# Stage one's products and stage two's token tiles of neighbouring batches, alternated one by one in the source

## The chip, the cores and the metric

The kernel runs on one core of a Trainium2 chip. The metric is the device time of one execution in microseconds (us); lower is better. TensorE (PE) multiplies into PSUM, VectorE (DVE), ScalarE (ACT) and GpSimd (POOL) work on the results, and SyncE (SP) issues the transfers. Each engine runs its own list of instructions in the list's order and waits on semaphores for the others.

## The reference, cut to what matters

Block-sparse attention over 4 batches of 768 tokens, then a mixture of 8 experts in which every token passes through every expert, with weights that a balancing loop makes:

```python
x = attention(q, k, v, sampled_blocks)          # 3072 tokens x 512
logits = x @ w_gate
P = np.exp(logits - logits.max())
for _ in range(8):                              # balance rows and columns
    P /= P.sum(1, keepdims=True) + 1e-09
    P /= P.sum(0, keepdims=True) + 1e-09
    P *= N / E
for e in range(E):                              # 8 experts
    h = np.maximum(x @ w1[e], 0.0)              # 512 -> 1024
    ye = h @ w2[e]                              # 1024 -> 512
    out += P[:, e:e + 1] * ye
```

## The kernel before, in words

The first 420 us or so are the attention. The rest is the experts, and the change is there. Every operand is held as a high and a low half in 16 bits, so that a product of two numbers takes three matmuls (high by low, low by high, high by high), and both matrix products of an expert are done by a scheme of seven products (`NP = 7`) of quarter matrices in place of eight.

The work goes by 32 steps `i`, an expert and a batch of 768 tokens each (`e, b = divmod(i, 4)`). A step has two stages.

- **Stage one** (`stage1(i, qi)`, `qi` from 0 to 3, a quarter each): seven products p0, p1, p5, p6, p3, p4, p2 in this order, each of six matmuls of 384 columns (L1200) into one of four PSUM banks (`ps_h`). DVE or ACT takes a product out of its bank: ACT for p0 (L1247), DVE for the others (`comb`, L1212, twice for p4). The results a1, r11, u3, c21 are made positive on ACT, added and subtracted on POOL (L1274, L1086), and split by `emit` into tiles for h: a high half by ACT (L1222), then a low half by DVE or POOL (L1226, L1232). There are 30 buffers for h; a step fills 28.
- **Stage two** (`stage2(i, p)`): for each of the seven products, in the order 1, 0, 5, 6, 3, 4, 2, three token tiles of twelve matmuls of 256 columns (L1325) into PSUM banks of another pool of four (`ps_y`). DVE (or ACT, for some of the first expert) adds each tile to the sum in SBUF (L1349, L1346). Products 5 and 6 go on in the bank of product 0, and 2 in that of 4, so DVE must have read a bank before the next product adds to it. A tile of stage two reads h of all four quarters.

In the names of the order below, `p3_12_0` is product 3 of step 12, quarter 0; `py_12_1_0` is the bank of stage two's product 1 of step 12, token tile 0; `h_24`, `acc_0`, `w2p_1` are buffers.

Stage one of step i+1 and stage two of step i have nothing to do with each other, and PE gets both. In the kernel before the source puts them in turns of whole blocks: stage two's products 1 and 0 (six tiles), quarter 0 (seven products), product 5 (three tiles), quarter 1, products 6 and 3, quarter 2, products 4 and 2, quarter 3.

Two things decide the order on each engine besides the source. `Slots` queues the small work of the other engines (high and low halves, weight splits) and places it by estimated costs at each `tick`, which comes after every product and every token tile. And the framework's scheduler then orders the instructions of each engine by its own estimate of when each will be ready, so that blocks of the source can be taken apart.

**The changeover.** After the fourth batch of an expert the weights of the next one take the place of the old ones. `split_w1` queues ACT's high halves (L1064) and DVE's low halves (L1068) of the seven w1 matrices at the last quarter of the last batch; `load_w(2, e + 1)` loads w2 (2 MB) into the buffer that w1 has just left, `scale_w` finds its largest magnitude in eight parts on ACT (L108) and a scale, and `split_w2` queues the halves (L1064, L1068) and POOL's sums (L1079). Steps 3, 7, 11, ... (b = 3) and the step after each are the changeover; in steps with b = 1 and 2 no weights are split.

Of the kernel before, what the change touches and what calls it, by code (L numbers as in the profile page):

```python
# [20 lines left out]
P = 128  # L21
# [19 lines left out]
PRE, LB2, LB1 = 0, 1, 1  # L41
# [13 lines left out]
def tile_sparse_attention_moe(  # L55
# [12 lines left out]
    B, H, S, D = q.shape  # L68
    NT, DM = out.shape
    NE, _, FF = w1.shape  # L70
# [6 lines left out]
    KF = FF // P  # L77
# [4 lines left out]
    FH = FF // 2  # L82
    CH = NC // 2
    TH = S // 2
    NP = 7
# [85 lines left out]
    wr = {}  # L171
# [879 lines left out]
    slots = Slots()  # L1051
# [131 lines left out]
    hs = {}  # L1183
# [7 lines left out]
    def stage1(i, qi, used=None):  # L1191
# [16 lines left out]
        def fresh(nm):  # L1208
            return upool.tile([P, TH], F32, tag="u", name=f"{nm}_{i}_{qi}")

        def comb(t, ps, other):
            nc.vector.scalar_tensor_tensor(  # L1212
                out=t, in0=ps, scalar=HDOWN, in1=other, op0=ALU.mult, op1=ALU.add
            )

        def emit(p, src, relu=False, delay=0):
            h = hfree.pop(0)
            hs[i, p, qi] = h
            key = ("h", i, p), i, qi

            def high():
                nc.scalar.activation(h[:, 0], src, AF.Relu if relu else AF.Copy)  # L1222

            def low():
                if relu:
                    nc.vector.scalar_tensor_tensor(  # L1226
                        out=h[:, 1], in0=src, scalar=0.0, in1=h[:, 0],
                        op0=ALU.max, op1=ALU.subtract,
                    )
                else:  # L1230
                    eng = nc.gpsimd if p in lop else nc.vector
                    eng.tensor_tensor(out=h[:, 1], in0=src, in1=h[:, 0], op=ALU.subtract)  # L1232
# [12 lines left out]

        a1 = fresh("a1")
        nc.scalar.activation(a1, product(0), AF.Copy, scale=HDOWN)  # L1247
# [7 lines left out]
        tick(1, 0)  # L1255
        u3 = fresh("u3")
        comb(u3, product(6), a1)
        tick(1, 0)
        slots.settle(i, qi - 1)
        c21 = fresh("c21")  # L1260
        comb(c21, product(3), u3)
        emit(1, c21, relu=True)
        tick(1, 1)
        p5 = product(4)
        comb(u3, p5, u3)
        comb(a1, p5, a1)
        nc.scalar.activation(u3, u3, AF.Relu)
        emit(3, u3)
        tick(2, 2)
        comb(a1, product(2), a1)  # L1270
        nc.scalar.activation(a1, a1, AF.Relu)  # L1271

# [13 lines left out]
        emit(5, r11, delay=SD[2])  # L1286
        emit(2, c21, delay=SD[3])
        tick(1, 1)

    READS = {  # L1290
        1: ((0, 0),),
# [12 lines left out]
    def stage2(i, p):  # L1304
        e, b = divmod(i, B)
# [8 lines left out]
        for ci in range(CH):  # L1314
# [63 lines left out]
    stage1(0, 0)  # L1378
    for part in split_w2(0, wr[2]):
        part()  # L1380
    stage1(0, 1)
    stage1(0, 2)
    stage1(0, 3)
    load_x(1)
    for step in xlast:
        slots.add(step, ("late", 0, 0), LATE, True, dve=1.0, act=0.8, pool=0.8)
    balance()
    queue_weight(0)
    for i in range(NI):
        e, b = divmod(i, B)  # L1390
        nxt = e + 1 < NE
        last = b == B - 1 and nxt
        more = i + 1 < NI
        if i == 2:
            finish_late()

        def quarter(qi):
            if more:
                swap = qi == FH // P - 1 and b == B - 2 and nxt
                stage1(i + 1, qi, split_w1(e + 1) if swap else None)  # L1400

        if b == LB2 and nxt:
            for p in range(NP):
                slots.need(("w2", e, p))
            if PRE:
                load_w(2, e + 1)
                scale_w(2, e + 1)
        if b == LB1 and nxt:
            slots.need(("scale", 2, e + 1))
            load_w(1, e + 1)  # L1410
            scale_w(1, e + 1)
            sum_w1(e + 1)
        stage2(i, 1)
        stage2(i, 0)
        if last:
            for p in range(NP):
                slots.need(("w1", e + 1, p))
            load_w(2, e + 1)
            parts = split_w2(e + 1, wr[2])
            scale_w(2, e + 1)  # L1420
            parts[0]()
            queue_weight(e + 1)
        quarter(0)
        stage2(i, 5)
        if last:
            parts[1]()
        quarter(1)
        stage2(i, 6)
        stage2(i, 3)
        if last:  # L1430
            parts[2]()
        quarter(2)
        stage2(i, 4)
        stage2(i, 2)
        if last:
            parts[3]()
        quarter(3)
        if i + 2 < NI:
            load_x(i + 2)

# [29 lines left out]
```

## Time and profile before

| | us |
|---|---|
| median of 3 runs | 2243.07 |
| their range | 2240.85 to 2245.97 |
| the profiled execution, whole | 2243.44 |
| its span, first to last instruction | 2241.5 |
| busy: PE / DVE / ACT / POOL | 2167.8 / 1696.3 / 1319.2 / 1320.5 |
| granted TensorE clock | 0.998 |

The table's busy times are unions of the instructions' spans. A matmul's span includes the way through the array, so a PE row that counts as busy is not necessarily at full rate; the rate is read from the distance between starts. "Idle before" in the views of PE is the time from the modelled end of a matmul to the start of the next.

### The profile page before, as it was taken

Reading aid. Unit: us, or ns where it says so; the run is one execution under the profiler, and the core shown is the slowest. Engines: PE = TensorE matmul, PEld = TensorE weight load, DVE = VectorE, ACT = ScalarE, POOL = GpSimd, SP = SyncE. Lnnn points to the kernel's source line nnn. Section 1 sums busy time; section 2 is a strip of 40 time slices with the busy share of each in tenths; the row PEclk is TensorE's granted clock in tenths of the full one; section 3 lists DMA queues with packets and bytes.
Section 4 is the critical chain, followed back from the end, with each engine's and each line's share of the span. In section 5 each row is a group of like instructions: output and inputs, shape, how many; then the busy total and the mean of one; then the engine's idle time right before and its main releaser. Section 6 shows DMA issues by size and latency. Waiting matters only on the chain.

```text
span 2241.5 us, 47250 instructions
## 1 busy us (share of the span) xinstructions
PE 2167.8 (97%) x18892; PEld 1598.0 (71%) x18892; DVE 1696.3 (76%) x2989; ACT 1319.2 (59%) x2443; POOL 1320.5 (59%) x1369
## 2 busy tenths in 40 slices
PE   6999999889999999999999999999999999999999
PEld 4777667567677777677767776777677767776777
DVE  7889999777877667866786678767876787678765
ACT  6988889764566555554555455545554555455442
POOL 3124456595568564856585658565856585658553
PEclk9999999999999999999999999999999999999999
DMA  7666866313121212121212121212121212121221
GB/s 166 141 147 148 206 130 145 116 57 116 50 88 51 88 50 88 50 88 50 88 50 88 51 88 50 88 50 88 50 88 50 88 50 88 50 88 57 78 79 50
DMA packets 195345, 192.35 MB, mean 86 GB/s; under 512 B 132124, under 2 KB 150580, under 8 KB 195124
## 3 DMA queue, kind: packets, MB, share of 16 engines
q1 hardware_dynamic: 194560, 189.30, 29.5%
q8 instruction: 147, 2.41, 0.4%
q14 instruction: 74, 0.61, 0.1%
q10 hardware_dynamic: 564, 0.03, 0.0%
HBM read 140.54 MB, written 17.30 MB: 70 GB/s over the span
## 4 chain that ended last, share of the span: by engine, by line
PE 60%; DVE 13%; POOL 10%; ACT 8%; issue 5%; DMA 4%; DVEq 0%; SPq 0%; POOLq 0%; ACTq 0%
PE py L1325 25%; PE p L1200 24%; DMA r<-in_moe_w_dram 3%; PE u L760 3%; POOL r L1079 2%; ACT h L1222 2%; DVE top L678 2%; PE t L705 2%; PE m L669 2%; PE m L672 2%; PE t L702 2%; POOL s L1274 2%; ACT unread L108 2%; POOL h L1232 2%; DVE attic L1068 1%
## 5 line engine op out<-in xcount | busy, mean ns | idle before, releaser
L1325 PE MATMUL py<-w2p,h 128*128 128x256 f16 x8064 | 952.5, 273 | 12.7 <-DVE acc L1349 4.6
L1325 PEld LDWEIGHTS <-h 128*128 128x128 f16 x8064 | 787.8, 98 | 154.6 <-issue 17.1
L1232 POOL TENSOR_TENSOR h<-u,h 128x384 f16<-128x384 f32 x128 | 124.8, 975 | 559.1 <-ACT h L1222 559.1
L1200 PEld LDWEIGHTS <-attic 128*128 128x128 f16 x3072 | 299.5, 98 | 206.1 <-issue 24.5
L1200 PE MATMUL p<-attic 128*128 128x384 f16 x2304 | 412.3, 326 | 16.5 <-DVE a L1212 10.2
L1200 PE MATMUL p<-arena 128*128 128x384 f16 x2304 | 416.3, 327 | 2.2 <-DVE u L1212 1.0
L1349 DVE SCALAR_TENSOR_TENSOR acc<-py,spare,acc 128x256 f32<-128x256 f32 (+1 forms) x588 | 295.3, 515 | 144.9 <-PE py L1325 142.8
L1222 ACT ACTIVATE h<-c 128x384 f16<-128x384 f32 x256 | 132.8, 522 | 320.4 <-DVE c L1212 262.8
L1200 PEld LDWEIGHTS <-arena 128*128 128x128 f16 x2304 | 225.8, 98 | 130.7 <-issue 4.6
L1212 DVE SCALAR_TENSOR_TENSOR a<-p,a 128x384 f32<-128x384 f32 x384 | 211.6, 551 | 22.6 <-PE p L1200 16.7
L678 DVE TENSOR_REDUCE top<-m 128x1 f32<-128x768 f32 x192 | 182.0, 952 | 31.2 <-PE m L672 30.8
L710 ACT ACTIVATE pe<-t,qk 128x768 int32<-128x768 f32 x192 | 172.1, 899 | 45.1 <-PE t L705 42.2
L1222 ACT ACTIVATE h<-s 128x384 f16<-128x384 f32 x128 | 67.1, 524 | 174.6 <-POOL s L1274 174.6
L1222 ACT ACTIVATE h<-r 128x384 f16<-128x384 f32 x256 | 131.7, 521 | 61.8 <-POOL r L1086 58.9
L1232 DVE TENSOR_TENSOR h<-s,h 128x384 f16<-128x384 f32 x128 | 105.5, 824 | 80.6 <-ACT h L1222 80.6
L1086 POOL TENSOR_TENSOR r<-s,r 128x384 f32<-128x384 f32 x128 | 154.0, 1203 | 10.0
L1086 POOL TENSOR_TENSOR c<-c,r 128x384 f32<-128x384 f32 x128 | 151.1, 1181 | 10.0
L1200 PE MATMUL p<-arena,attic 128*128 128x384 f16 x768 | 146.2, 326 | 5.5 <-ACT a L1247 4.7
L1274 POOL TENSOR_TENSOR s<-a,u 128x384 f32<-128x384 f32 x128 | 140.9, 1101 | 16.7 <-ACT a L1271 16.6
L1232 POOL TENSOR_TENSOR h<-r,h 128x384 f16<-128x384 f32 x128 | 134.7, 1052 | 18.3 <-ACT h L1222 16.3
L1079 POOL TENSOR_TENSOR r<-r 128x256 f32<-128x256 f32 (+1 forms) x106 | 119.1, 1148 | 30.9 <-DVE arena L1068 30.9
L669 PE MATMUL m<-kt,qt 128*128 128x512 f16 (+1 forms) x384 | 127.8, 333 | 9.0 <-DMA kt<-ks 6.8
(205 smaller groups left out, 3671.8 us busy)
## 6 DMA issues: line engine op xcount, KB each, us to landing
arena<-xd SPq DMA_DIRECT2D x128, 384.0 KB, 3.9
attic<-xd SPq DMA_DIRECT2D x96, 384.0 KB, 4.2
r<-in_moe_w_dram SPq DMA_DIRECT2D x16, 2048.0 KB, 8.6
arena<-in_q_dram SPq DMA_DIRECT2D x16, 384.0 KB, 4.0
arena<-in_k_dram SPq DMA_DIRECT2D x16, 384.0 KB, 4.3
arena<-in_v_dram SPq DMA_DIRECT2D x4, 1536.0 KB, 8.3
xd<-xs_t SPq DMA_DIRECT2D x16, 384.0 KB, 3.1
out_dram<-acc SPq DMA_DIRECT2D x48, 128.0 KB, 1.7
```

Source lines behind the costliest of these rows:

```text
L669: nc.tensor.matmul(sc[:, lo:hi], lhsT=qt[:, 0, c], rhs=ka[:, lo:hi], start=True, stop=False)
L678: nc.vector.tensor_reduce(out=tops[n][:, c : c + 1], in_=sc[:, :S], axis=AX.X, op=ALU.max)
L710: nc.scalar.activation(pe, sc[:, :S], AF.Exp, bias=EXP_SHIFT, scale=qk[n // 2][3])
L1079: lambda c=c: Pinned.gpsimd.tensor_tensor(out=out[:, c], in0=x[:, c], in1=y[:, c], op=op),
L1086: nc.gpsimd.tensor_tensor(out=out, in0=x, in1=y, op=ALU.subtract)
L1200: nc.tensor.matmul(ps, lhsT=w1p[p][:, l, kc, fs], rhs=xp[p][:, r, kc], start=(kc == 0 and m == 0), stop=(kc == KH - 1 and m == 2),)
L1212: nc.vector.scalar_tensor_tensor(out=t, in0=ps, scalar=HDOWN, in1=other, op0=ALU.mult, op1=ALU.add)
L1222: nc.scalar.activation(h[:, 0], src, AF.Relu if relu else AF.Copy)
L1232: eng.tensor_tensor(out=h[:, 1], in0=src, in1=h[:, 0], op=ALU.subtract)
L1274: nc.gpsimd.tensor_tensor(out=s1, in0=a1, in1=u3, op=ALU.add)
L1325: nc.tensor.matmul(py, lhsT=hs[i, p, kc][:, l, tsl], rhs=w2p[p][:, r, kc], start=(old is None and kc == 0 and m == 0), stop=(kc == KF // 2 ...
L1349: nc.vector.scalar_tensor_tensor(out=dst, in0=src, scalar=c, in1=dst, op0=ALU.mult, op1=ALU.add)
```

## The change

`stage1` and `stage2` become generators that yield after each product and each token tile. The loop over the steps starts stage two's tiles of step i three tiles ahead (`LEAD = 3`), and then takes products of step i+1 and tiles of step i in turn, 28 products against the 18 tiles that are left. The order of the products within each stage is what it was. The new weights' work hangs on the generators: w2's load stands after the sixth tile and the product that precedes the seventh, which makes seven products ahead of it in the source where there were none. The buffers for h are taken from the list when the high half is made, not when it is queued, and are given back after the last tile of a product.

```diff
         def emit(p, src, relu=False, delay=0):
-            h = hfree.pop(0)
-            hs[i, p, qi] = h
             key = ("h", i, p), i, qi
 
             def high():
+                h = hs[i, p, qi] = hfree.pop(0)
                 nc.scalar.activation(h[:, 0], src, AF.Relu if relu else AF.Copy)
 
             def low():
+                h = hs[i, p, qi]
...
         nc.scalar.activation(a1, product(0), AF.Copy, scale=HDOWN)
         tick(0, 1)
+        yield
         r11 = fresh("r11")
...
             slots.tick(1.31, 0.47 if k is not None else 0.74)
-        for kc in range(KF // 2):
-            hfree.append(hs.pop((i, p, kc)))
+            if ci == CH - 1:
+                for kc in range(KF // 2):
+                    hfree.append(hs.pop((i, p, kc)))
+            yield
...
+    ORDER2 = (1, 0, 5, 6, 3, 4, 2)
+    LEAD = 3
...
+    def products(i):
+        e, b = divmod(i, B)
+        for qi in range(FH // P):
+            swap = qi == FH // P - 1 and b == B - 1 and e + 1 < NE
+            yield from stage1(i, qi, split_w1(e + 1) if swap else None)
+
+    def outputs(i):
+        e, b = divmod(i, B)
+        last = b == B - 1 and e + 1 < NE
+        for n, p in enumerate(ORDER2):
+            yield from stage2(i, p)
+            if last and n == 1:
+                for x in range(NP):
+                    slots.need(("w1", e + 1, x))
+                load_w(2, e + 1)
+                parts = split_w2(e + 1, wr[2])
+                scale_w(2, e + 1)
+                parts[0]()
+                queue_weight(e + 1)
+            elif last and n in (2, 4, 6):
+                parts[n // 2]()
...
-        stage2(i, 1)
-        stage2(i, 0)
-        if last:
-            for p in range(NP):
-                slots.need(("w1", e + 1, p))
-            load_w(2, e + 1)
...
-        quarter(0)
-        stage2(i, 5)
...
-        quarter(3)
+        two = outputs(i)
+        if i + 1 == NI:
+            run(two)
+            break
+        one = products(i + 1)
+        n1, n2 = NP * FH // P, NP * CH
+        for n in range(LEAD):
+            next(two)
+        done = 0
+        for n in range(n1):
+            next(one)
+            want = (n + 1) * (n2 - LEAD) // n1
+            for _ in range(want - done):
+                next(two)
+            done = want
+        run(one)
+        run(two)
         if i + 2 < NI:
             load_x(i + 2)
```

What the scheduler makes of it, on the engines for which PE waits in the changeover to expert 3 (steps 11 to 13). Up to the middle of step 1 PE's list is the same row for row. From there on, of the 672 tiles of stage two, 598 stand in one piece on PE, where 431 did, and PE's list changes between products and tiles 1125 times, where it did 825 times. All instructions are the same in number and shape.

ACT's list in step 12, from the search for w2's largest magnitude (`unread`) to the drain of p0 of quarter 2 (`a1_12_2<-p0_12_2`), before:

```order
L108 ACTIVATE unread_80,mx_w2_3_15976<-r2_3_15973 128x512 x2
L1222 ACTIVATE h_21_8093<-s1_12_1_16180 128x384
L1222 ACTIVATE h_4_8076<-a1_12_1_16104 128x384
L1222 ACTIVATE h_15_8087<-r11_12_1_16116 128x384
L1222 ACTIVATE h_13_8085<-c21_12_1_16149 128x384
L1247 ACTIVATE a1_12_2_16277<-p0_12_2_16278 128x384
```

And the same place now:

```order
L108 ACTIVATE unread_80,mx_w2_3_16052<-r2_3_16049 128x512
L1277 ACTIVATE a1_12_1_16070<-a1_12_1_16070 128x384
L1247 ACTIVATE a1_12_2_16226<-p0_12_2_16227 128x384
L1221 ACTIVATE h_1_8073<-s1_12_1_16205 128x384
L108 ACTIVATE unread_80,mx_w2_3_16052<-r2_3_16049 128x512
L1221 ACTIVATE h_3_8075<-a1_12_1_16070 128x384
```

The drain of p0 stood behind four high halves, which take POOL's results of the quarter before; it now stands ahead of them.

DVE's list in step 13, quarter 1, around the drain of p5 (`a1_13_1<-p5_13_1`), before:

```order
L1212 SCALAR_TENSOR_TENSOR r11_13_1_16790<-p1_13_1_16791,a1_13_1_16777 128x384
L1232 TENSOR_TENSOR h_14_8086<-a1_13_0_16648,h_14_8086 128x384
L1068 SCALAR_TENSOR_TENSOR w2p_4_8069<-t1_3_15975,sw2_3_15978,w2p_4_8069 128x1024
L1349 SCALAR_TENSOR_TENSOR acc_0_8102<-py_12_0_0_16601,spare_6_16491,acc_0_8102 128x256
L1232 TENSOR_TENSOR h_7_8079<-r11_13_1_16790,h_7_8079 128x384
L1349 SCALAR_TENSOR_TENSOR acc_0_8102<-py_12_0_1_16617,spare_6_16491,acc_0_8102 128x256
L1349 SCALAR_TENSOR_TENSOR acc_0_8102<-py_12_0_2_16632,spare_6_16491,acc_0_8102 128x256
L1212 SCALAR_TENSOR_TENSOR a1_13_1_16777<-p5_13_1_16801,a1_13_1_16777 128x384
```

And now:

```order
L1068 SCALAR_TENSOR_TENSOR w2p_5_8070<-r2_3_16049,sw2_3_16054,w2p_5_8070 128x1024
L1212 SCALAR_TENSOR_TENSOR r11_13_1_16773<-p1_13_1_16774,a1_13_1_16746 128x384
L1212 SCALAR_TENSOR_TENSOR a1_13_1_16746<-p5_13_1_16787,a1_13_1_16746 128x384
L1232 TENSOR_TENSOR h_5_8077<-s1_13_0_16724,h_5_8077 128x384
L1212 SCALAR_TENSOR_TENSOR u3_13_1_16810<-p6_13_1_16811,a1_13_1_16746 128x384
```

Six rows stood between the drains of p1 and p5, a weight split and three additions of tiles among them; now none does.

DVE's list at the start of step 13, where the first weights that stage two of expert 3 needs are split (`w2p_1`), before:

```order
L1212 SCALAR_TENSOR_TENSOR a1_12_3_16455<-p2_12_3_16528,a1_12_3_16455 128x384
L1068 SCALAR_TENSOR_TENSOR w2p_1_8066<-r2_3_15973,sw2_3_15978,w2p_1_8066 128x1024
L1212 SCALAR_TENSOR_TENSOR r11_13_0_16658<-p1_13_0_16659,a1_13_0_16648 128x384
L1212 SCALAR_TENSOR_TENSOR a1_13_0_16648<-p5_13_0_16671,a1_13_0_16648 128x384
```

And now:

```order
L1356 SCALAR_TENSOR_TENSOR acc_3_9931<-py_11_4_2_16428,spare_5_13892,acc_3_9931 128x256
L1212 SCALAR_TENSOR_TENSOR r11_13_0_16612<-p1_13_0_16613,a1_13_0_16603 128x384
L1232 TENSOR_TENSOR h_24_8096<-s1_12_3_16523,h_24_8096 128x384
L1212 SCALAR_TENSOR_TENSOR a1_13_0_16603<-p5_13_0_16639,a1_13_0_16603 128x384
L1068 SCALAR_TENSOR_TENSOR w2p_1_8066<-r2_3_16049,sw2_3_16054,w2p_1_8066 128x1024
```

The split of `w2p_1` has moved from ahead of step 13's first drains to behind those of p1 and p5. On PE the first tiles that read it stood behind four products of step 13, and stand behind six now. On ACT, 110 of the high halves carry a wait for PE (for the last reads of the buffer's old content), where 61 did.

More of the change, by code (lines that the diff above doesn't have):

```diff
@@ L1253, in stage1 @@
         tick(1, 2)
+        yield
         comb(a1, product(5), a1)
         tick(1, 0)
+        yield
         u3 = fresh("u3")
@@ L1258, in stage1 @@
         tick(1, 0)
+        yield
         slots.settle(i, qi - 1)
@@ L1263, in stage1 @@
         tick(1, 1)
+        yield
         p5 = product(4)
@@ L1269, in stage1 @@
         tick(2, 2)
+        yield
         comb(a1, product(2), a1)
@@ L1288, in stage1 @@
         tick(1, 1)
+        yield
     READS = {
@@ L1377, in tile_sparse_attention_moe, with run @@
     NI = NE * B
-    stage1(0, 0)
+    ORDER2 = (1, 0, 5, 6, 3, 4, 2)
+    LEAD = 3
+    def run(steps):
+        for _ in steps:
+            pass
+    run(stage1(0, 0))
     for part in split_w2(0, wr[2]):
         part()
-    stage1(0, 1)
-    stage1(0, 2)
-    stage1(0, 3)
+    for qi in range(1, FH // P):
+        run(stage1(0, qi))
     load_x(1)
@@ L1391, in tile_sparse_attention_moe @@
         nxt = e + 1 < NE
-        last = b == B - 1 and nxt
-        more = i + 1 < NI
         if i == 2:
             finish_late()
[L1397 to L1400, printed above, removed]
         if b == LB2 and nxt:
```

20 lines of the change are left out of this document (1 added, 19 removed).

## The prediction, as it was put on record before the run

> **What bounds the kernel now.** The page's head and first row come first.
>
> ```profile
> span 2241.5 us, 47250 instructions
> PE 2167.8 (97%) x18892; PEld 1598.0 (71%) x18892; DVE 1696.3 (76%) x2989; ACT 1319.2 (59%) x2443; POOL 1320.5 (59%) x1369
> ```
>
> PE is the bound, but 97% doesn't say at what rate it works. The timeline of PE in a step without weight work (start, length, engine, line, instruction, count) gives the rate by the distance between starts.
>
> ```profile
> 779.82 6.28 PE L1325 MATMUL py<-w2p,h 128*128 128x256 f16 x56
> 785.93 3.09 PE L1200 MATMUL p<-arena 128*128 128x384 f16 x18
> 788.86 1.14 PE L1200 MATMUL p<-arena,attic 128*128 128x384 f16 x6
> 789.83 0.71 PE L1325 MATMUL py<-w2p,h 128*128 128x256 f16 x5
> 790.38 3.09 PE L1200 MATMUL p<-attic 128*128 128x384 f16 x18
> ```
>
> 56 matmuls of a tile take 785.93 - 779.82 = 6.11 us, 0.109 each; 18 of products take 2.93, 0.163 each. So a product of six costs 0.98 us and a tile of twelve 1.31. The last two rows tell what a change of stage costs: five matmuls of a tile between two products take 0.55, 0.110 each, so nothing. Next the windows view, 110 us each, two without weight work (the first and the last) and two changeovers.
>
> ```profile
> core 0: us, PE busy (x) PEld busy (x) DVE busy (x) ACT busy (x) POOL busy (x), PEclk, DMA share, GB/s
> 755.00:865.00 110.00, 110.00 (x846) 82.54 (x845) 74.57 (x138) 60.26 (x123) 65.26 (x63) 1.00 0.16 52
> 865.00:975.00 110.00, 106.86 (x808) 78.57 (x806) 87.02 (x150) 65.39 (x129) 76.16 (x73) 1.00 0.22 74
> 1090.00:1200.00 110.00, 106.68 (x809) 78.48 (x807) 87.02 (x150) 61.71 (x122) 78.02 (x73) 1.00 0.22 76
> 1202.00:1312.00 110.00, 110.00 (x847) 82.60 (x845) 73.64 (x137) 53.76 (x112) 64.28 (x62) 1.00 0.16 53
> ```
>
> Without weight work PE never stands: nothing can be won there. A changeover has 38 matmuls fewer in the same time, which at 110 / 846 = 0.13 us each is 4.9 us lost, although DVE is busy for 87.0 of 110 us only. So these are waits, not a full engine. The list of PE's waits from 865 us on (us in total, times, longest) names them.
>
> ```profile
> PE p L1200 <- DVE a L1212: 8.0, 6, 1.3
> PE p L1200 <- ACT a L1247: 4.7, 5, 0.9
> PE py L1325 <- DVE acc L1349: 4.6, 10, 1.0
> PE p L1200 <- ACT attic L1064: 2.3, 5, 0.5
> PE py L1325 <- DVE h L1226: 1.2, 6, 0.2
> PE p L1200 <- ACT arena L1064: 0.5, 1, 0.5
> PE p L1200 <- DVE r L1212: 0.4, 1, 0.4
> ```
>
> Most are waits for a PSUM bank that DVE or ACT has not emptied in time (a, acc, r: 17.7 us, 22 times); weights come next (attic, arena: 2.8, 6 times), and low halves of h (1.2, 6 times). The view counts from the modelled end of a matmul, and that is late: a product's last matmul lasts 1.14 - 5 x 0.163 = 0.33 us where the next may follow after 0.163. Each wait is thus about 0.16 us longer than shown.
>
> The same wait, in the same step of two changeovers five apart, gives the whole loss:
>
> ```profile
> 947.17 1.14 PE L1200 MATMUL p<-attic 128*128 128x384 f16 x6 [1.33 <-DVE a L1212]
> ...
> 2071.21 0.97 PE L1200 MATMUL p<-attic 128*128 128x384 f16 x5 [1.34 <-DVE a L1212]
> ```
>
> (2071.21 - 947.17) / 5 = 224.8 us per expert. Its work is four steps of 168 matmuls of products and 252 of tiles: 672 x 0.1628 + 1008 x 0.1091 = 219.4. So 5.4 us are lost per changeover, and six changeovers from 865 us on hold 32.5. Of these the waits explain 17.7 + 22 x 0.16 = 21.2 for banks, 2.8 + 6 x 0.16 = 3.8 for weights, 1.2 + 6 x 0.16 = 2.2 for h; 5.3 are left for waits too short to show.
>
> **The change, part by part.** *Banks.* Two changeover waits, one on ACT and one on DVE:
>
> ```profile
> 1124.41 1.20 POOL L1086 TENSOR_TENSOR c<-c,r 128x384 f32<-128x384 f32 x1
> ...
> 1125.64 0.52 ACT L1222 ACTIVATE h<-c 128x384 f16<-128x384 f32 x1 [0.75 <-POOL c L1086]
> 1126.07 0.47 ACT L1247 ACTIVATE a<-p 128x384 f32<-128x384 f32 x1
> ...
> 1126.59 0.97 PE L1200 MATMUL p<-arena,attic 128*128 128x384 f16 x5 [0.94 <-ACT a L1247]
> ```
>
> ACT drains p0 only after four high halves that wait for POOL, and p6, which needs that bank, stands for 0.94 + 0.16 = 1.1 us. In the new order the drain is ahead of those halves: its own 0.47 us is all that is left. Besides, between p0 and p6 there is now a tile of 1.31 us, so the same lateness of 1.1 would be covered even without the move. The wait on DVE is alike:
>
> ```profile
> 1164.67 0.90 DVE L1232 TENSOR_TENSOR h<-s,h 128x384 f16<-128x384 f32 x1 [2.90 <-ACT h L1222]
> ...
> 1166.77 2.01 DVE L1068 SCALAR_TENSOR_TENSOR w2p<-t,sw,w2p 128x1024 f16<-128x1024 f32 x1
> ...
> 1170.68 0.54 DVE L1212 SCALAR_TENSOR_TENSOR a<-p,a 128x384 f32<-128x384 f32 x1
> ```
>
> p5's drain starts at 1170.68 behind a low half, a weight split and three tiles; it now follows the drain of p1 directly. PE meets the banks with four products in a row (3 x 0.98 = 2.9 us between a bank's uses) in the old order and mostly with one or two tiles among them (4.2 to 5.6) in the new. Bounds: at most all 21.2 us go, at least those at the two shown places (6 and 5 of the 22, 8.0 + 4.7 + 11 x 0.16 = 14.5) shrink by half, 7. I take 19 of 21.2, near the upper end, because both the order and the distance help. The low half of h that stage two's first tile waits for comes from p3 of the last quarter; between the two PE now has two tiles of the old step more (2.6 us) against waits of 0.2 + 0.16 each: 2.2 go, or none.
>
> *Weights.* The waits for w1 I leave as they are, since an old matrix still can't be overwritten before its last product: 3.8 stay (0 to 8). Where the new w2p_1 is read, a wait could appear: with 0 at the start of step 13, p1 ends at 1.95, and DVE then does a drain, a low half, a drain and the split. The rows for these, with that of a tile's addition (by shape; the mean of one in ns is the second number behind the first bar):
>
> ```profile
> L1349 DVE SCALAR_TENSOR_TENSOR acc<-py,spare,acc 128x256 f32<-128x256 f32 x504 | 233.8, 477 | 139.4 <-PE py L1325 137.2 <-ACT acc L1333 1.5
> L1212 DVE SCALAR_TENSOR_TENSOR a<-p,a 128x384 f32<-128x384 f32 x384 | 211.6, 551 | 22.6 <-PE p L1200 16.7
> ...
> L1232 DVE TENSOR_TENSOR h<-s,h 128x384 f16<-128x384 f32 x128 | 105.5, 824 | 80.6 <-ACT h L1222 80.6
> ...
> L1068 DVE SCALAR_TENSOR_TENSOR w2p<-r,sw,w2p 128x1024 f16<-128x1024 f32 x48 | 66.1, 1379 | 12.5 <-ACT w2p L1064 12.5
> ```
>
> 1.95 + 0.16 + 0.55 + 0.82 + 0.55 + 1.38 = 5.4 us. PE reaches the first matmul that needs it after six products and one matmul, 6 x 0.98 + 0.11 = 6.0. It is in time by 0.6 us; I take 0 (bounds 0 and 0.7, the split at its longest of 2.01).
>
> *Short waits.* Of the 5.3 half goes, 2.7 (0 to 5).
>
> *The first expert.* Its waits up to 865 us, the two largest:
>
> ```profile
> PE py L1325 <- ACT acc L1346: 3.9, 5, 1.1
> PE cs L1169 <- DVE spare L1163: 3.1, 3, 2.2
> ```
>
> The first two quarters of step 1 keep their order, and with them about half of these. I take 3.5 of 3.9 + 3.1 + 8 x 0.16 = 8.3 as gone (0 to 8).
>
> *Costs.* 300 more changes of stage at 0 each (up to 0.005, 1.5 us, would not show). Taking h's buffer later has no instruction. 49 more high halves on ACT wait for PE; that is the third rival.
>
> *Sum.* 19 + 2.2 + 0 + 2.7 + 3.5 = 27.4 us less. Against the profiled execution's own 2243.44 (span 2241.5 and 1.9 around it; 0.4 above the median of 2243.07) this is 2216. With the low ends (7 + 0 - 4 - 1.5 and some) it is hardly 12 less, 2231; with the high ends (21 + 2 + 4 + 5 + 8 = 40) 2203.
>
> **The rivals.** *The waits come back as a backlog of DVE* (0.11). DVE's work is unchanged. In the w1 split, from the end of p1 of quarter 3 of the old expert's last step to p3 of the new one, DVE now has ten drains (5.5), seven splits, nine tiles at 0.48 (4.3) and five low halves (4.1), with splits at 1.38 some 23.6 us, against 20.6 us of PE (nine tiles and nine products, 11.8 + 8.8). That holds, since PE comes to the last split's first use only after p3, a tile, p4, two matmuls and seven of a tile more (4.4 us), at 25.0. But the split has also been slower:
>
> ```profile
> L1068 DVE SCALAR_TENSOR_TENSOR w2p<-t,sw,w2p x8: 1760/2016/2021, 493.1 to 2066.7; 128x1024 f16<-128x1024 f32 x8
> ```
>
> At a median of 2.016 in place of 1.38, seven cost 4.5 us more, 28.1, 3.1 us late; six times that is 19, with the first expert's 22: 2235 to 2238. For it: these rows are of the same shape as the 48 above and never under 1.76. Against: they are 8 beside those 48. The Trainium skill ("SBUF — State Buffer", section "SBUF: two separate sides") speaks for this rival: a DVE instruction with two inputs in SBUF and a GpSimd instruction lock each other out for a whole instruction. The two durations above agree with that; if interleaving made every split meet POOL, the sum would be this rival's.
>
> *w2 comes later: slower* (0.06). In the source its load has moved behind seven more products, 7 x 0.98 = 6.8 us. The chain behind it has no room:
>
> ```profile
> ACT unread L108 <- DMA r<-in_moe_w_dram: 15.8, 8, 3.3
> ...
> r<-in_moe_w_dram SPq DMA_DIRECT2D x16, 2048.0 KB, 8.6
> ```
>
> ACT waited for the landing eight times, once for each of the eight w2. Two more products run ahead of the first tile (2.0 us), so 4.9 us would be lost in each of seven changeovers, 34: 2216 + 34 = 2250. It decides from (27.4 + 4.5) / 7 = 4.6 us per changeover on. Against it:
>
> ```profile
> 1101.31 3.13 DVE L1068 SCALAR_TENSOR_TENSOR attic<-r,sw,attic 128x1024 f16<-128x1024 f32 x2
> 1104.51 0.38 SPq L177 DMA_DIRECT2D r<-in_moe_w_dram  x1
> ```
>
> The load leaves 0.1 us after the last w1 split has read the buffer, not when the source comes to it, and SP has nothing else ahead of it. That split stands at most two products later than before.
>
> *ACT stands in its queue* (0.04). A high half that waits for PE holds all of ACT behind it.
>
> ```profile
> ACT h L1222 <- PE py L1325: 3.5, 5, 0.8
> ```
>
> 49 more at the longest of these, 0.8, would be 39 us if all reached PE: 2216 + 39 = 2255. Against it: the drain behind such a half has 4.2 us or more until its bank is needed.
>
> *It does not take effect* (0.03), as the scheduler already mixed the stages: 2243. The order speaks against it.
>
> **How the numbers follow.** The forecast has 0.76, its own range 2203 to 2231. The range to hold 8 in 10 goes on to 2238 for the backlog. About 0.2%, 4.5 us, is what a measurement of this kernel can tell from no change; so faster means below 2238.6. Half of the backlog case counts as faster, half as the same: faster 0.82, same 0.05 + 0.03 = 0.08, slower 0.10.
>
> **What would show it.** Right: between the same points of two changeovers about 221 us per expert in place of 224.8, PE's waits for a (DVE, ACT) and acc from 865 us on all but gone, those for attic at about 2 us, the steps without weight work as full as before, DVE's total the same. Banks wrong: these lines are there with other steps. Weights wrong: new lines "py <- DVE w2p" or "py <- ACT w2p" of a microsecond or more in each changeover. Rival on ACT: "ACT h <- PE py" in tens of us, and PE waiting for ACT a.

## The result, and the profile after

| | before | after |
|---|---|---|
| median, us (runs on the same chip) | 2244.52 | 2212.48 |
| range, us | 2240.85 to 2246.11 | 2211.47 to 2214.77 |
| ratio, 95% interval | 1 | 0.9861 (0.9846 to 0.9875) |
| the profiled execution; its span, us | 2243.44; 2241.5 | 2212.46; 2210.7 |
| granted TensorE clock | 0.998 | 0.997 |

The change makes the kernel 1.4% faster, 30.8 us by the spans of the two profiled executions. The profile page's head and first row:

```profile
span 2210.7 us, 47146 instructions
PE 2159.4 (98%) x18892; PEld 1599.2 (72%) x18892; DVE 1741.3 (79%) x2989; ACT 1317.0 (60%) x2443; POOL 1334.8 (60%) x1369
```

The same matmuls, and PE's busy share rises by a point only; as before, that row doesn't show where the time went. The windows view does (110 us each, one without weight work, then two changeovers; the number in brackets is the count of instructions):

```profile
755.00:865.00 110.00, 110.00 (x845) 82.45 (x843) 78.72 (x138) 60.20 (x123) 68.84 (x63) 1.00 0.17 51
865.00:975.00 110.00, 109.47 (x837) 81.56 (x836) 91.83 (x155) 64.92 (x130) 76.54 (x75) 1.00 0.28 90
1090.00:1200.00 110.00, 109.45 (x837) 81.59 (x836) 89.70 (x152) 62.00 (x129) 74.09 (x72) 1.00 0.28 89
```

Without weight work PE does what it did (845 matmuls, 846 before), so nothing was won there, and 300 more changes of stage cost nothing. A changeover's window has 837 in place of 808, although DVE is busier in it than before (91.8 of 110 us against 87.0): DVE was not short of time, only late at some places. PE's whole list of waits from 865 us on is now two rows:

```profile
PE p L1200 <- DVE attic L1068: 2.1, 5, 0.4
PE p L1200 <- ACT a L1247: 0.5, 1, 0.5
```

The bank waits (a on DVE and ACT, acc, r: 17.7 us, 22 times) are gone but for one of 0.5, and so are the six for low halves of h. The wait that is left, in the same step of two changeovers four apart, gives the period:

```profile
1091.60 1.15 PE L1200 MATMUL p<-attic 128*128 128x384 f16 x6 [0.41 <-DVE attic L1068]
...
1973.15 1.15 PE L1200 MATMUL p<-attic 128*128 128x384 f16 x6 [0.42 <-DVE attic L1068]
```

(1973.15 - 1091.60) / 4 = 220.4 us per expert, where it was 224.8 and its work is 219.4. Six times 4.4 is 26.4 of the 30.8 us; the other 4.4 lie before 865 us. At the place that the prediction showed on ACT, the drain of p0 in step 12, quarter 2, the timeline now reads:

```profile
1121.58 0.49 ACT L1247 ACTIVATE a<-p 128x384 f32<-128x384 f32 x1 [1.02 <-PE p L1200]
```

ACT waits there for PE, where PE had waited 0.94 us for ACT. And on DVE, step 13, quarter 1:

```profile
1151.69 0.55 DVE L1212 SCALAR_TENSOR_TENSOR r<-p,a 128x384 f32<-128x384 f32 x1
1152.35 0.56 DVE L1212 SCALAR_TENSOR_TENSOR a<-p,a 128x384 f32<-128x384 f32 x1
1153.21 0.91 DVE L1232 TENSOR_TENSOR h<-s,h 128x384 f16<-128x384 f32 x1 [0.31 <-ACT h L1221]
```

The two drains follow each other, and the low half that waits for ACT stands behind them.

### The profile page after: what moved, and what is told of

Same layout as the page of the kernel before. It is cut to its first block, busy times and chain, and to the rows that moved or that the text cites. A ratio compares the mean times of both kernels' runs of the same rounds, so it can differ in the third digit from the quotient of the medians.

```text
span 2210.7 us, 47146 instructions
## 1 busy us (share of the span) xinstructions
PE 2159.4 (98%) x18892; PEld 1599.2 (72%) x18892; DVE 1741.3 (79%) x2989; ACT 1317.0 (60%) x2443; POOL 1334.8 (60%) x1369
## 4 chain that ended last, share of the span: by engine, by line
PE 77%; DVE 10%; ACT 4%; POOL 4%; issue 3%; DMA 1%; SPq 0%; DVEq 0%; POOLq 0%; ACTq 0%
PE py L1332 33%; PE p L1200 33%; PE u L760 3%; PE t L705 2%; PE t L702 2%; PE m L669 2%; PE m L672 2%; DVE top L678 2%; DVE a L1212 1%; DVE attic L1068 1%; POOL s L1280 1%; DVE h L1232 1%; DVE u L1212 1%; ACT h L1221 1%; DVE pl L721 1%
## 5 line engine op out<-in xcount | busy, mean ns | idle before, releaser
L1332 PE MATMUL py<-w2p,h 128*128 128x256 f16 x8064 | 972.9, 273 | 3.8 <-DVE h L1226 1.3
L1232 POOL TENSOR_TENSOR h<-u,h 128x384 f16<-128x384 f32 x128 | 128.4, 1003 | 534.8 <-ACT h L1221 534.7
L1200 PE MATMUL p<-attic 128*128 128x384 f16 x2304 | 422.9, 327 | 8.4 <-DVE attic L1068 2.5
L1212 DVE SCALAR_TENSOR_TENSOR a<-p,a 128x384 f32<-128x384 f32 x384 | 211.1, 550 | 17.8 <-PE p L1200 5.0
L1232 DVE TENSOR_TENSOR h<-s,h 128x384 f16<-128x384 f32 x128 | 112.8, 881 | 135.4 <-ACT h L1221 135.3
L1086 POOL TENSOR_TENSOR c<-c,r 128x384 f32<-128x384 f32 x128 | 161.2, 1259 | 10.0
L1232 POOL TENSOR_TENSOR h<-r,h 128x384 f16<-128x384 f32 x128 | 146.4, 1144 | 2.6 <-ACT h L1221 2.0
L1086 POOL TENSOR_TENSOR a<-a,r 128x384 f32<-128x384 f32 x128 | 128.7, 1005 | 10.0
L702 PE MATMUL t<-qt,kt 128*128 128x512 f16 (+1 forms) x384 | 126.5, 329 | 6.2 <-DVE top L678 5.3
```

Of the source, the lines that this page charges most:

```text
L702: nc.tensor.matmul(sc[:, lo:hi], lhsT=kt[:, 0, c], rhs=qa[:, lo:hi], start=True, stop=False)
L1086: nc.gpsimd.tensor_tensor(out=out, in0=x, in1=y, op=ALU.subtract)
L1200: nc.tensor.matmul(ps, lhsT=w1p[p][:, l, kc, fs], rhs=xp[p][:, r, kc], start=(kc == 0 and m == 0), stop=(kc == KH - 1 and m == 2),)
L1212: nc.vector.scalar_tensor_tensor(out=t, in0=ps, scalar=HDOWN, in1=other, op0=ALU.mult, op1=ALU.add)
L1332: nc.tensor.matmul(py, lhsT=hs[i, p, kc][:, l, tsl], rhs=w2p[p][:, r, kc], start=(old is None and kc == 0 and m == 0), stop=(kc == KF // 2 ...
```

## The experiments

The theory was that PE's waits in the changeover are waits for PSUM banks behind other work in the in-order lists of DVE and ACT, made by the weight splits, and that alternation hides them. Rivals were that alternation itself runs faster, that late buffers or the load's place do the work, and that any finer mixing would do. All ratios are to the kernel before, run on the same chip.

**Without the splits.** `queue_split` does nothing for experts after the first, in the kernel before (e5) and in the changed one (e6); those experts multiply with the first one's halves.

```diff
     def queue_split(dst, src, key, delay=1):
+        if key[1]:
+            return
```

> The kernel before without the splits of w1 and w2 for the experts after the first (no high and low halves of new weights on ACT and DVE, 14 of each per changeover; loads, magnitudes and POOL's sums stay, the output is made with the first expert's weights). If the changeover's waits come from these splits delaying the drains: the loss of 5.4 us per changeover goes, 2244 - 33 to 36 = 2208 to 2213, and hardly a wait of PE from 865 us on. If the waits come from the blocks themselves: 2235 or more.

> The same left out of the changed kernel. It loses only 0.9 to 1 us per changeover, so 5 to 7 us less than the changed kernel: 2205 to 2208. If the change had hidden more than waits (PE at a better rate), it would stay well below the kernel before without splits; by my theory the two come within 5 us, the rest being the first expert's waits.

Measured: 2209.33 us, ratio 0.9857 (0.9843 to 0.9872), and 2206.92 us, 0.9847 (0.9832 to 0.9862). Neither profile has a wait of PE from 865 us on. Without the splits the old blocks are as good as the alternation to 2.4 us, so alternation has no better rate of its own. The splits cost the kernel before 32.3 us (2241.59 - 2209.33, measured side by side), and the changed one 3 to 6: 5.6 by the medians (2212.48 - 2206.92), which were taken at different times, 3.1 by the two ratios. So the change hides most of what the splits cost. The two runs do not part the waits for banks from the waits for the new halves.

**Banks.** In the kernel before, one bank goes from stage two to stage one (e8); in the changed one, stage one has three banks (e9).

```diff
-    ps_h = mpool("ps_h", 4, space=PSUM)
-    ps_y = mpool("ps_y", 4, space=PSUM)
+    ps_h = mpool("ps_h", 5, space=PSUM)
+    ps_y = mpool("ps_y", 3, space=PSUM)
```

```diff
-    ps_h = mpool("ps_h", 4, space=PSUM)
+    ps_h = mpool("ps_h", 3, space=PSUM)
```

> The kernel before with five PSUM banks for products and three for tiles, in place of four and four. Theory 1 (the time between two uses of a bank counts): PE's waits for DVE a and ACT a (12.7 us from 865 us on) fall by most, those for DVE acc rise; 2230 to 2243 in all. Theory 2 (the drains' place in their queues counts, not the banks): the waits for a stay at 10 us or more.

> The changed kernel with three banks for products in place of four: two products and one or two tiles between two uses of a bank, 3.3 to 4.6 us, between the 2.9 of the blocks and the 4.2 to 5.6 of the change. Theory 1: a part of the bank waits comes back, 2215 to 2225. Theory 2: no change, 2210 to 2215.

Measured: e8 2249.08 us, 1.0044 (1.0027 to 1.006), 6 us above theory 1's range; e9 2218.03 us, 0.9896 (0.9881 to 0.9911). PE's waits from 865 us on, first the first row of e8, then the whole list of e9:

```profile
PE py L1325 <- DVE acc L1349: 24.7, 15, 3.2
```

```profile
PE p L1200 <- DVE a L1212: 5.9, 6, 1.3
PE p L1200 <- DVE attic L1068: 1.0, 5, 0.2
PE py L1332 <- DVE acc L1356: 0.9, 1, 0.9
```

With a fifth bank the products' waits for banks (13.1 us of the 17.7) vanish from the list, and stage two's grow from 4.6 to 24.7: they are bank waits, and the lateness only changes pools. With one bank fewer one wait per changeover comes back in the changed kernel, some 6 us in all (5.5 by the medians, 5.6 by the spans). The lists of DVE and ACT are nearly those of the changed kernel there (2882 of 2989 and 2374 of 2443 rows in the same order), so the distance between two uses of a bank does some of the hiding.

**The three parts of the change apart.** With the generators but in the old turns of blocks: w2's load after seven products, as the change has it (e1), or after the sixth tile, as before (e10). And the alternation with the load after the sixth tile, which puts five products ahead of it (e4). h is taken late in all three; alternation with buffers taken when queued needs more of them than the 30 there are, so there is no run of it.

```diff
-        for n in range(LEAD):
-            next(two)
...
+        for tiles in (6, 3, 6, 6):
+            for _ in range(tiles):
+                next(two)
+            for _ in range(NP):
+                next(one)
```

```diff
-            yield from stage2(i, p)
+            tiles = stage2(i, p)
+            for _ in range(CH - 1):
+                next(tiles)
+                yield
+            next(tiles)
+            if not (last and n == 1):
+                yield
+            for _ in tiles:
+                pass
             if last and n == 1:
...
                 queue_weight(e + 1)
+                yield
```

> The changed kernel with the old turns of whole blocks (6 tiles, 7 products, 3 tiles, 7 products, 6 tiles, 7 products, 6 tiles, 7 products); h's buffers taken late, the generators and the later place of w2's load stay. Theory 1 (the alternation is what helps, since it puts tiles between two uses of a bank): as slow as the kernel before, 2240 to 2248, with PE's waits for DVE a, ACT a and DVE acc from 865 us on at 15 to 20 us again. Theory 2 (taking h late, and with it another order on ACT and DVE, is what helps): 2212 to 2225.

> The old turns of whole blocks, written with the generators, as in e1_blocks, but with w2's load and the queueing of its split directly after the sixth tile, where the kernel before had them; only the late taking of h's buffers then stands between this and the kernel before. Theory A: e1_blocks lost 40 us against before because in blocks the load's place behind seven products makes w2's chain late, and taking buffers late is neutral: 2238 to 2250, PE's waits for the spread of w2's magnitude (all_w) gone or under 3 us, its waits for banks (a, acc) at 12 to 20 us as before. Theory B: late buffers themselves cost in blocks, since ACT's high halves stand in other places: 2265 to 2285, and the waits for all_w stay small while others make the loss.

> In the changed kernel w2's load and the queueing of its work stand directly after the sixth tile, one turn earlier in the source. If the load's time hangs on the last split of w1 alone (the load leaves when the buffer is free): no change, 2209 to 2216. If the source's place counts, by the third part of the prediction's rivals: faster by up to 1 us per changeover, 2205.

| median, us; ratio, 95% interval | load after the sixth tile | load seven products in |
|---|---|---|
| blocks | e10: 2243.37; 1.0001 (0.9992 to 1.0011) | e1: 2283.63; 1.0169 (1.0146 to 1.0192) |
| alternating | e4: 2229.19; 0.9932 (0.9916 to 0.9948) | changed kernel: 2212.48; 0.9861 (0.9846 to 0.9875) |

Late buffers alone change nothing (e10): the rows of ACT, DVE and POOL stand in the order of before, all of them. The later load costs 40 us in blocks and saves 17 in alternation, which the expectations of e1 and e4 did not have. The first rows of PE's waits from 865 us on, in e1 and in e10:

```profile
PE all_w L114 <- DVE ma_w L194: 17.9, 6, 5.4
PE p L1200 <- DVE a L1212: 9.9, 6, 2.5
```

```profile
PE p L1200 <- DVE a L1212: 8.0, 6, 1.3
PE p L1200 <- ACT a L1247: 4.6, 5, 0.9
```

In blocks with the late load PE reaches the spread of w2's magnitude (`all_w`, a transpose in PE's own list) before the search is done, and stands in front of it, 3.0 us per changeover: the prediction's second rival, at a place that it hadn't named. In e4 the loss is elsewhere, and in many small pieces. One of them begins on ACT. ACT, then DVE in step 13:

```profile
1150.85 0.51 ACT L1221 ACTIVATE h<-c 128x384 f16<-128x384 f32 x1
1156.40 1.15 ACT L1064 ACTIVATE w2p<-r,sw 128x1024 f16<-128x1024 f32 x1 [5.04 <-POOL r L1079]
1157.46 0.51 ACT L1221 ACTIVATE h<-c 128x384 f16<-128x384 f32 x1
```

```profile
1158.00 0.56 DVE L1226 SCALAR_TENSOR_TENSOR h<-c,h 128x384 f16<-128x384 f32 x1 [1.36 <-ACT h L1221]
1158.47 0.55 DVE L1212 SCALAR_TENSOR_TENSOR u<-p,u 128x384 f32<-128x384 f32 x1
...
1163.65 0.90 DVE L1232 TENSOR_TENSOR h<-s,h 128x384 f16<-128x384 f32 x1 [1.44 <-ACT h L1221]
1164.48 0.47 DVE L1356 SCALAR_TENSOR_TENSOR acc<-py,spare,acc 128x256 f32<-128x256 f32 x1
1164.87 0.54 DVE L1212 SCALAR_TENSOR_TENSOR r<-p,a 128x384 f32<-128x384 f32 x1
```

A high half of w2 stands on ACT 5.04 us for POOL's sum of quarter matrices (L1079); the high half of h behind it is late, DVE's low half waits for that, and drains stand behind the low half. In ACT's list of waits from 865 us on this one row is 30.3 us in six times in e4, 12.7 in the kernel before, and absent in the changed kernel. But ACT's wait is not PE's loss. By the distances between PE's starts, PE loses 0.33 us at the drain of a and 0.38 at that of r behind it (until 1159.55 and 1165.47), of some 2.2 us that this changeover has over that of the changed kernel. The greater part of the rest lies ahead of ACT's long wait: 0.27 at the spread of the magnitude, 0.47 at the halves of w2, 0.46 at a tile's addition.

**The grain and the lead.** Turns of four products, tiles first (e3_by_four); of two products (e3_by_two); stage two four or two tiles ahead (e7); four tiles ahead with the load one tile later, seven products in again (e11).

```diff
-        for n in range(LEAD):
-            next(two)
-        done = 0
-        for n in range(n1):
-            next(one)
-            want = (n + 1) * (n2 - LEAD) // n1
-            for _ in range(want - done):
+        for n in range(0, n1, 4):
+            want = LEAD + (n + 4) * (n2 - LEAD) // n1
+            for _ in range(want - (n and LEAD + n * (n2 - LEAD) // n1)):
                 next(two)
-            done = want
+            for _ in range(4):
+                next(one)
```

```diff
             next(one)
+            if (n + 1) % 2:
+                continue
             want = (n + 1) * (n2 - LEAD) // n1
```

```diff
-    LEAD = 3
+    LEAD = 4
```

The second of the two e7 kernels has `LEAD = 2` in that line. e11 has `LEAD = 4` and this:

```diff
-            yield from stage2(i, p)
-            if last and n == 1:
+            tiles = stage2(i, p)
+            if last and n == 2:
+                next(tiles)
+                yield
+            if not (last and n == 2):
+                yield from tiles
+            if last and n == 2:
...
                 queue_weight(e + 1)
-            elif last and n in (2, 4, 6):
+                yield from tiles
+                parts[1]()
+            elif last and n in (4, 6):
                 parts[n // 2]()
```

> Turns of four products and two or three tiles in place of one by one. A product's bank is used again by the fourth product after it, so each reuse still has two or three tiles in between. Theory 1a (only the time between two uses of a bank counts): as fast as the changed kernel, 2210 to 2218. Theory 1b (DVE's and ACT's work must come evenly, one product or tile at a time): about half of the gain, 2222 to 2234. Theory 2: 2212 to 2220, the alternation is indifferent.

> The changed kernel with the alternation in pairs: two products, then the tiles due. Theory A, the distance between two uses of a bank, falling with the size of the turn: 2216 to 2228, between the changed kernel and the turns of four (2245), with the rest in waits of products for a and u on DVE. Theory B, the places that the scheduler's list happens to give to low halves and weight splits among DVE's drains decide, and every source order but one draws anew: no reason for a place between; anything from 2212 to 2250, and the waits differ in kind (low halves ahead of drains, or the spread of w2's magnitude) and not only in size.

> LEAD = 4 in the changed kernel: one more tile of the old step ahead of the products, so that each product of a new expert comes 1.3 us later against DVE's splits of w1. What is left of the loss in a changeover is PE waiting for the low halves of w1 (0.58 + 0.30 us each). Theory: these waits go, 7 x 0.9 = 6 us, 2206 to 2208. Rival: they are set by when the splits begin, which moves as well: 2210 to 2214.

> The changed kernel with stage two two tiles ahead in place of three (LEAD 2). Theory A, distance between bank uses: the alternation is the same, so within 0.2% of the changed kernel, 2208 to 2217. Theory B, the places in DVE's list decide, as one tile more (2229) suggests: a loss of some 10 us again, 2220 to 2235, with 1.5 to 3 us lost per changeover in waits for banks (acc, a, r) behind low halves that wait for ACT.

> Four tiles ahead, as in e7_lead4, but w2's load and the queueing of its split one tile later in the source, after the seventh. That gives it seven products ahead of it, as in the changed kernel (three tiles ahead, 2212), where e7_lead4 and e4_load_early had five (both 2229, spans 2227.3). Theory A, it is the load's place among the products that cost those two 17 us, since the search for w2's magnitude on ACT then ran from 21.0 to 27 us behind the start of the changeover in place of 33, and w2's low halves crowded ahead of DVE's drains: 2208 to 2216, the search over 11 to 12 us again, PE's waits for acc and for the spread of the magnitude gone. Theory B, the fourth tile ahead is itself what cost e7_lead4 its 17 us, and the agreement with e4_load_early is chance: 2224 to 2232, waits for acc at some 10 us as before.

| | median, us | ratio, 95% interval | us per expert |
|---|---|---|---|
| e3_by_four (one of its ten executions took 4577.21 us) | 2244.81 | 1.0 (0.999 to 1.0009) | 225.2 |
| e3_by_two | 2234.44 | 0.9957 (0.9943 to 0.9972) | 222.8 |
| e7_lead4 | 2229.33 | 0.9935 (0.9916 to 0.9954) | 223.3 |
| e11_lead4_load | 2220.19 | 0.9896 (0.9874 to 0.9917) | 221.5 |
| changed kernel (lead 3) | 2212.48 | 0.9861 (0.9846 to 0.9875) | 220.4 |
| e7_lead2 | 2210.49 | 0.9853 (0.9838 to 0.9867) | 220.2 |

The last column is the distance between the first matmuls of steps 12 and 16. PE's waits from 865 us on: the first row of e3_by_four, the first of e3_by_two, the first two of e7_lead4, the first three of e11:

```profile
PE p L1200 <- DVE ma_w L200: 7.8, 6, 1.5
```

```profile
PE py L1332 <- DVE acc L1356: 10.7, 7, 1.7
```

```profile
PE py L1332 <- DVE acc L1356: 10.4, 12, 1.6
PE all_w L114 <- DVE ma_w L194: 3.9, 6, 0.8
```

```profile
PE p L1200 <- DVE attic L1068: 3.4, 5, 0.7
PE py L1332 <- ACT w2p L1064: 2.3, 6, 0.4
PE py L1332 <- DVE w2p L1068: 1.2, 6, 0.2
```

Turns of four win nothing, which no expectation had, and turns of two a quarter (8.4 of some 32 us), less than the theory of distance had put. What the scheduler makes of these sources is not what they look like: PE's list changes between products and tiles 679 times in e3_by_four, 825 times in the kernel before, 875 in e3_by_two and 1125 in the changed kernel. Distance between two uses of a bank does not explain them either. Between a product and the fourth after it, which needs its bank, less than one tile's twelve matmuls stand in 276 of 864 cases before and in 34 in the changed kernel, but also in only 49 in e3_by_four, 20 in e3_by_two and 6 in e4. Each of the slower orders leaves waits at places of its own.

e7_lead4 came out above what either theory had. ACT's wait for POOL's sums is as long as in e4 (30.1 us in six times), but PE does not lose there: in this changeover PE stands last at 1149.22, and ACT's wait begins then. The large wait of PE is earlier. PE, then ACT:

```profile
1146.93 1.47 PE L1332 MATMUL py<-w2p,h 128*128 128x256 f16 x12 [1.57 <-DVE acc L1356]
```

```profile
1154.22 1.15 ACT L1064 ACTIVATE w2p<-r,sw 128x1024 f16<-128x1024 f32 x1 [5.03 <-POOL r L1079]
```

DVE and POOL ahead of the large wait:

```profile
1142.31 0.56 DVE L1232 TENSOR_TENSOR h<-s,h 128x384 f16<-128x384 f32 x1 [1.74 <-ACT h L1221]
...
1144.31 0.90 DVE L1232 TENSOR_TENSOR h<-a,h 128x384 f16<-128x384 f32 x1 [0.31 <-ACT h L1221]
1145.28 1.20 DVE L1232 TENSOR_TENSOR h<-r,h 128x384 f16<-128x384 f32 x1
1146.41 0.47 DVE L1356 SCALAR_TENSOR_TENSOR acc<-py,spare,acc 128x256 f32<-128x256 f32 x1
```

```profile
1139.06 1.71 POOL L1079 TENSOR_TENSOR r<-r,t 128x256 f32<-128x256 f32 x1
1140.72 1.00 POOL L1280 TENSOR_TENSOR s<-a,u 128x384 f32<-128x384 f32 x1
1141.68 0.73 POOL L1079 TENSOR_TENSOR r<-r 128x256 f32<-128x256 f32 x1
1142.36 1.36 POOL L1086 TENSOR_TENSOR a<-a,r 128x384 f32<-128x384 f32 x1
```

PE stood for the last of DVE's rows, a tile's addition, behind three low halves and two drains. The first two low halves wait for ACT's high halves, these for POOL's results s and a, and in POOL's list each of the two stands behind a sum of w2's quarter matrices (L1079). Giving this kernel the later load (e11) takes the waits for acc down to 0.4 us: the place of the load was their cause, as theory A had it, though the rows in front of this addition are low halves of h, not of w2. But the time comes down by 9 us, not 17, between the two theories. PE now reaches the new w2 earlier in the changeover (its first tile 55.2 us behind the first matmul of step 12, in the changed kernel 57.7) and waits for its halves in every one, which neither theory had. The four executions range from 2217.14 to 2223.54 us; the profiled one, of 2222.94, stands once for 4.8 us at 484 us, ahead of these changeovers (the last section shows at what), so a part of the distance from the changed kernel lies there.

Two tiles ahead is as good as three: the two intervals overlap, so it isn't called better.

## Why the prediction held

*The bound* was read rightly: steps without weight work full, six changeovers of 5.4 us lost each. The forecast was 221 us per expert, and 220.4 came; 23.9 us from the changeovers (19 + 2.2 + 2.7), and 26.4 came.

*Banks.* 19 of 21.2 was still a little low: one wait of 0.5 + 0.16 is left. Of the two reasons given, the runs bear out the order in the lists. At the two places that the prediction read, the rows came as read. The distance on PE counts too (e9, some 6 us), but it was told too simply: in the old order only 54 of 864 uses of a product's bank come with no tile's matmul in between, and e3_by_four and e4 have the distance without the gain. "Alternation hides bank waits" as a rule would have missed e3_by_four by 30 us. Some luck was in it as well. The prediction read two places, and e4, e7_lead4 and e3_by_two lose 17 to 22 us against this order at other places, at the spread, at the halves of w2 and at the additions of tiles. The prediction did not go through those places for its own order, which happens to have no such wait.

*Weights.* "3.8 stay" was right in size (2.1 + 5 x 0.16 = 2.9 by the list, 4.4 with the waits too short for it, by the distances between PE's starts), but not in kind: the wait was for ACT's high halves and is for DVE's low halves now. The place is the one where the first rival looked for a backlog of DVE:

```profile
1089.32 0.56 DVE L1232 TENSOR_TENSOR h<-r,h 128x384 f16<-128x384 f32 x1 [0.75 <-ACT h L1221]
1089.80 0.55 DVE L1212 SCALAR_TENSOR_TENSOR a<-p,a 128x384 f32<-128x384 f32 x1
1090.27 1.27 DVE L1068 SCALAR_TENSOR_TENSOR attic<-r,sw,attic 128x1024 f16<-128x1024 f32 x1
```

The split of p4's matrix ends at 1091.54, and PE's wait of 0.41 ends with it at 1091.60. Behind it PE stands 0.14 more for the split of p2's. With 0.16 on each that is 0.9 us in this changeover, where the rival had put 3.1, and it is most of what is left over the run without splits. It is not a backlog of a full engine: in the first of these rows DVE had itself stood 0.75 us for ACT. At w2p_1 no wait came, as taken, but both ends of the margin were misread. The split ended 6.0 us behind step 13's first product (1139.79 - 1133.78), not 5.4. And PE's list has, behind the six products, one matmul of each of w2p_1's three tiles, which read the high half, then ten with w2p_0; the first that needs the low half starts at 7.3 us, not 6.0. In e11, where PE comes earlier, it waits for both halves.

*The first expert* was put at 3.5 and came out at 4.4, the rest of the spans' difference; 0.4 of it is there already at the last row that PE's two lists share (495.62 us before, 495.26 now). Its largest wait, for ACT's additions of tiles, fell from 3.9 us in five times to 0.7 in one; the one for the column sums of the balancing loop (cs) from 3.1 to 1.2.

*Costs at nothing.* Changes of stage and late buffers cost nothing (the 845 matmuls above; e10). ACT's waits for PE in high halves of h, the third rival, were 3.5 us in five times and are not in the list any more.

*w2 comes later* did not happen in the changed kernel, for the reason given: the load waits for the last w1 split, and leaves 11.8 us behind the first matmul of step 12, where it left 12.2 behind. That reason belongs to this order, though, not to the load: in blocks it leaves after 21.1 us (e1), and each expert takes 229.3 us in place of 224.4 (e10). The 4.9 us are what the rival was priced at, though the wait at the spread is only 3.0 of them, so that the agreement is in part chance.

*What was wrong* is, besides the margin at w2p_1, one line of "what would show it": DVE's total was to be the same, and it rose by 1741.3 - 1696.3 = 45.0 us. PE's waits for DVE's splits are only the 0.9 us per changeover above, and no run shows how much of that comes from the rise. One sum was wrong as well: the low end of the range is given as 7 + 0 - 4 - 1.5 "and some", hardly 12 us; these terms make 1.5, and a range that followed them would have reached to 2242. The forecast's own sum and the high end add up.

## What to carry to other kernels

An engine that is 76% busy can still hold TensorE up, if drains of PSUM banks stand in its in-order list behind work that waits for a third engine; look there first when windows of the same length hold different counts of matmuls. Interleaving two independent streams can give the drains more time, but what it is worth lies in the lists that the scheduler makes of it: here seven interleaved orders ran from 2210 to 2245 us. So read the lists of the very kernel, and try the neighbours (the lead, the place of a load) before the result of one order is taken for a rule.

## What the runs showed of the hardware

DVE's 45 us came from the same 2989 instructions, and not from those that read PSUM (the 384 drains into a: 211.6 us before, 211.1 now). Four groups that take both inputs from SBUF make up the sum, by shape (busy us, then the mean of one in ns), before and after; the groups h<-s and w2p<-r of before are in the prediction:

```profile
L1232 DVE TENSOR_TENSOR h<-a,h 128x384 f16<-128x384 f32 x128 | 116.5, 910 | 18.6 <-ACT h L1222 18.0
L1232 DVE TENSOR_TENSOR h<-r,h 128x384 f16<-128x384 f32 x128 | 96.3, 753 | 34.0 <-ACT h L1222 33.9
```

```profile
L1232 DVE TENSOR_TENSOR h<-a,h 128x384 f16<-128x384 f32 x128 | 124.7, 974 | 5.1 <-ACT h L1221 5.1
L1232 DVE TENSOR_TENSOR h<-r,h 128x384 f16<-128x384 f32 x128 | 114.6, 896 | 19.1 <-ACT h L1221 18.9
L1232 DVE TENSOR_TENSOR h<-s,h 128x384 f16<-128x384 f32 x128 | 112.8, 881 | 135.4 <-ACT h L1221 135.3
L1068 DVE SCALAR_TENSOR_TENSOR w2p<-r,sw,w2p 128x1024 f16<-128x1024 f32 x48 | 77.4, 1614 | 3.1 <-ACT w2p L1064 3.0
```

8.2 + 18.3 + 7.3 + 11.3 = 45.1 us; the changes of the other groups, of some 5 us and less, cancel. Of the 384 low halves at L1232, those that meet no POOL instruction take 0.56 us in both kernels (53 of them before, 19 now), and the others 0.87 before and 0.94 now. The splits w2p<-t, on which the first rival's price rested, show it best. Before, all eight met a POOL instruction, and their median was 2.016 us. Now seven of the eight meet none and take 1.27 us each, and the eighth, which does, takes 1.76:

```profile
L1068 DVE SCALAR_TENSOR_TENSOR w2p<-t,sw,w2p 128x1024 f16<-128x1024 f32 x8 | 10.6, 1331 | 0.0
```

The longest case is PE's stand of 4.8 us in e11. The drain that it waits for stood behind a split that took 6.06 us, while POOL's instructions followed one another with hardly a gap from 477.2 to 489.7 us:

```profile
482.75 6.06 DVE L1068 SCALAR_TENSOR_TENSOR w2p<-r,sw,w2p 128x1024 f16<-128x1024 f32 x1 [1.83 <-ACT w2p L1064]
```

The same split took 1.93 us in the kernel before and 5.11 in e10, where every row of DVE and POOL stands in the order of before, so this can come without any change of order.

All this agrees with the lock between DVE and GpSimd which the prediction cited from the Trainium skill ("SBUF — State Buffer", section "SBUF: two separate sides"), where it stands for a GpSimd instruction that reads SBUF, as POOL's sums here do. Where the two engines work side by side more of the time, DVE's instructions get longer without any more of them. No run here took POOL's work away to show it alone.
